# One block around an attention and feed-forward kernel, ordered with the tool's other timing model

## The chip, the cores and the metric

The kernel runs on one core of one Trainium2 chip. The metric is the time of one execution on the device, in microseconds, as the median of several executions.

## The reference

Block-causal attention for 8 batches with 8 heads, 576 positions and 64 columns per head, and behind it a feed-forward layer over all 8 x 576 = 4608 tokens, with 512 columns in and out and 2048 between. Scores are masked in blocks of 64: a position sees its own block and those before it. The weights of the feed-forward arrive as 64-bit floats.

```python
scores = scale * np.matmul(q, k.transpose(0, 1, 3, 2))
scores = np.where(block_i >= block_j, scores, -1000000000.0)
scores = scores - np.max(scores, axis=-1, keepdims=True)
attn = np.exp(scores)
attn = attn / (np.sum(attn, axis=-1, keepdims=True) + 1e-09)
x = np.matmul(attn, v)        # then heads side by side: (4608, 512)
h = x @ w_in
g = np.where(h >= 1, h, np.where(h <= -1, 0.0, (h + 1) ** 2 / 4.0))
out = g @ w_out
```

## The kernel before, in words

Three pieces of work are written as Python generators, and a loop at the end of the function interleaves them.

Attention goes by pairs of heads: 8 batches x 4 pairs = 32 pairs, eight steps each (`attention_steps`). A pair's q and k are loaded in natural layout (`load`, L276 to L300), split into a high and a low part on DVE and POOL (`split_q` L310 and L311, `split_k` L320 and L321, `split_v` L335 and L336), and turned by PE transposes (`turned`, matmul L346; ACT copies the result out at L351, and a DMA at L357 copies one half to other partitions; the last block has L365, L370 and L371). `scores` multiplies (L391 and L394), takes the row maximum on DVE (L414), the exponential with its sum on ACT (L418), and scales on DVE (L400, L401, L424); `scores_last` does the same for the last block (L438 to L450). From the second batch on, the scaled scores `pr` are copied by a DMA into a tile of the type that PE transposes faster (`as_float32r`, L239 for the second batch and L246 behind it). `turn` and `turn_last` transpose them (L461, or L463 in the first batch) and copy them out on ACT and DVE (L454, L456). `weighted` multiplies with v (L500), and the result becomes `xh` and `xl`, the high and low parts of the feed-forward's input (L522, L523, L535, L536, L565, L566). The first two batches use simpler forms of some of these steps.

The feed-forward goes by 9 chunks of 512 tokens, and in each by 16 blocks of 128 of the 2048 columns. `ffn_in` runs twelve matmuls into one PSUM bank (L646), then the activation over ACT, DVE, DVE, ACT and POOL (L655, L656, L659, L660, L661), and loads the block's second weights (L663). `ffn_out` runs eight and four matmuls into four banks (L670, L675); behind the last block of a chunk the banks are copied out (L683, L685) and stored (L687). A chunk can begin only when the attention of its tokens' batch is done, for all four pairs.

The weights are prepared in 64 pieces of 128x256 (`convert`): a load (L160), two steps on ACT (L165, L166), three on DVE (L167, L170, L173), an addition on POOL (L179), a copy on ACT (L181), a subtraction on POOL (L183), and for the second weights a store to DRAM (L209). The pieces are used from the first chunk on.

The order. The loop at the end draws one attention step, then some weight pieces, and from step 36 on one step of the feed-forward (`ffn_in` or `ffn_out` in turn). So from then on a batch of attention stands beside a chunk of the feed-forward: chunk 0 beside batch 1, up to chunk 6 beside batch 7; chunks 7 and 8 come alone. This written order isn't yet that of the chip. The ordering tool runs the traced program in a simulated time of its own: on each engine, and on the queue of SP, which issues all DMAs, it takes the instruction written earliest among those that are ready by its timing model. What comes out is one fixed list for each engine, which the engine then works off in order, waiting at each instruction for the semaphores that the tool has put there. How good the lists are depends on how near the tool's timing model is to the chip. Buffers are few in places: one bank for `ph`, four for `po`, three for the other PSUM tiles (and `po` banks too, in the first 36 steps), two buffers each for `t`, `gh`, `gl` and `wo`.

Of the kernel before, what the change touches and what calls it, by code (L numbers as in the profile page):

```python
# [23 lines left out]
def block_attn_then_ffn(  # L24
# [59 lines left out]


    ident_f = ffn.tile([P, 512], F32, tag="t", name="ident_f")[:, :P]
    make_identity(nc, ident_f)
    ident_r = const.tile([P, P], F32R, tag="ident", name="ident_r")
    nc.vector.tensor_copy(ident_r, ident_f)
    ident = ident_r.bitcast(F32)  # L90

    xh = const.tile([P, NCC, RING], F32R, tag="xh", name="xh")
    xl = const.tile([P, NCC, RING], F32R, tag="xl", name="xl")
    wih = const.tile([P, NCC, DF], F32R, tag="wih", name="wih")
    wil = const.tile([P, NCC, DF], F32R, tag="wil", name="wil")
    wo_split = dram.tile([NFC, P, 2, DM], F32, tag="wo_split", name="wo_split")
# [3 lines left out]
    qa = const.tile([P, 2, QW], F32R, tag="qa", name="qa")  # L100
    qb = const.tile([P, 2, QW], F32R, tag="qb", name="qb")
    ka = const.tile([P, 2, S], F32R, tag="ka", name="ka")
    kb = const.tile([P, 2, S], F32R, tag="kb", name="kb")

    def last_blocks(t_):

        view = t_[:, :, SM : SM + BLK]
        if t_.shape[2] == S:
            return view
        part, (_, two), cols = view.ap  # L110
        return bass.AP(tensor=view.tensor, offset=view.offset, ap=[part, [QW + BLK, two], cols])


    mrow = att1.tile([NTL, 2, S], F32R, tag="pb0", name="mrow")


    pcs = [const.tile([P, 2, BLK], F32R, tag=f"pcs{i}", name=f"pcs{i}") for i in range(2)]
    vsr = [const.tile([P, NTL + 1, 2, D], F32R, tag=f"vsr{j}", name=f"vsr{j}") for j in range(2)]

    mtmp = ffn.tile([P, 512], F32, tag="t", name="mtmp")  # L120
    msel = ffn.tile([P, 512], F32, tag="t", name="msel")
    nc.vector.memset(mtmp, 0.0)
    nc.vector.memset(msel[:NTL], 0.0)
    nc.gpsimd.affine_select(
        out=msel[:NTL, : NTL * BLK].rearrange("p (t c) -> p t c", c=BLK),
        in_=msel[:NTL, : NTL * BLK].rearrange("p (t c) -> p t c", c=BLK),
        compare_op=ALU.not_equal, fill=1.0, base=0,
        pattern=[[-1, NTL], [0, BLK]], channel_multiplier=1,
    )
    sel = msel[:NTL, : NTL * BLK].rearrange("p (t c) -> p t c", c=BLK)  # L130
    for side in range(2):
        nc.vector.tensor_copy(mrow[:, side, :512], mtmp[:NTL, :512])
        nc.vector.tensor_copy(mrow[:, side, 512:S], mtmp[:NTL, : S - 512])
    rows = mrow[:, :, :SM].rearrange("p s (t c) -> p s t c", c=P)
    nc.vector.tensor_copy(rows[:, 0, :, :BLK], sel)
    nc.vector.tensor_scalar_mul(rows[:, 1, :, BLK:], sel, MASKED)
    for t_ in (qa, qb):
        nc.vector.tensor_copy(
            t_[:, :, SM:], mtmp[:, : 2 * (QW - SM)].rearrange("p (h c) -> p h c", h=2)
        )  # L140
    for t_ in pcs:
        nc.vector.tensor_copy(t_[BLK:], mtmp[BLK:, : 2 * BLK].rearrange("p (h c) -> p h c", h=2))
    for t_ in vsr:
        nc.vector.tensor_copy(
            t_[BLK:, NTL, :, :], mtmp[BLK:, : 2 * D].rearrange("p (h c) -> p h c", h=2)
        )
    for j in range(2):
        nc.sync.dma_start(qa[D:KA, j, :S].bitcast(F32), mrow[:, 0, :].bitcast(F32))
        nc.sync.dma_start(ka[D:KA, j, :].bitcast(F32), mrow[:, 1, :].bitcast(F32))


    def convert(n, source, hi, lo, done):

        if n < BORROW and n % 2:
            bits = ffn.tile([P, CW, 2], I32, tag="t", name="bits")
            work = ffn.tile([P, 2, CW], F32, tag="gl", name="work")
        else:
            bits = conv.tile([P, CW, 2], I32, tag="bits", name="bits")
            work = conv2.tile([P, 2, CW], F32, tag="work", name="work")
        nc.sync.dma_start(bits, source.bitcast(I32).rearrange("p (n t) -> p n t", t=2))  # L160
        top, mag = work[:, 0, :], work[:, 1, :].bitcast(U32)
        low = bits[:, :, 0]


        nc.scalar.mul(top, bits[:, :, 1].bitcast(F32), 2.0**-112)  # L165
        nc.scalar.mul(low, low.bitcast(U32), 2.0**-29)  # L166
        nc.vector.tensor_scalar(  # L167
            out=top, in0=top, scalar1=F32_TOP, scalar2=-F32_TOP, op0=ALU.min, op1=ALU.max
        )
        nc.vector.tensor_scalar(  # L170
            out=mag, in0=top.bitcast(U32), scalar1=3, scalar2=None, op0=ALU.logical_shift_left
        )
        nc.vector.scalar_tensor_tensor(  # L173
            out=mag, in0=top.bitcast(U32), scalar=0x80000000, in1=mag,
            op0=ALU.bitwise_and, op1=ALU.bitwise_or,
        )
        yield
        w32 = mag.bitcast(I32)
        nc.gpsimd.tensor_tensor(out=w32, in0=w32, in1=low, op=ALU.add)  # L179
        w32 = w32.bitcast(F32)  # L180
        nc.scalar.copy(hi(), w32)  # L181
        yield
        nc.gpsimd.tensor_tensor(out=lo(), in0=w32, in1=hi().bitcast(F32), op=ALU.subtract)  # L183
        if done:
            done()

    def weight_pieces():

        for f0 in range(0, DF, CW):
            fs = slice(f0, f0 + CW)  # L190
            for cc in range(NCC):
                yield (
                    w_in[cc * P : (cc + 1) * P, fs],
                    lambda cc=cc, fs=fs: wih[:, cc, fs], lambda cc=cc, fs=fs: wil[:, cc, fs], None,
                )
            for fc in range(f0 // P, (f0 + CW) // P):
                ws = {}

                def part(w, d0, ws=ws):
                    if not ws:  # L200
                        ws[0] = ffn.tile([P, 2, DM], F32R, tag="wo", name="ws")
                    return ws[0][:, w, d0 : d0 + CW]

                for d0 in range(0, DM, CW):
                    yield (
                        w_out[fc * P : (fc + 1) * P, d0 : d0 + CW],
                        lambda p_=part, d0=d0: p_(0, d0), lambda p_=part, d0=d0: p_(1, d0),
                        None if d0 + CW < DM else
                        lambda fc=fc, ws=ws: nc.sync.dma_start(wo_split[fc], ws[0].bitcast(F32)),  # L209
                    )  # L210

    def prepare_weights():

        live = []
        for n, piece in enumerate(weight_pieces()):
            live = [c for c in live + [convert(n, *piece)] if next(c, True) is None]
            yield
        for _ in range(LAG):
            live = [c for c in live if next(c, True) is None]
            yield  # L220
# [3 lines left out]
    spare = {"n": 0, "of": []}  # L224

    def as_float32r(src, plain):

        if plain:
            if not spare["of"]:
                spare["of"] = [t_[:, :NTL, :, :].rearrange("p t h d -> p (t h d)") for t_ in vsr]  # L230
                spare["of"].append(att1.tile([P, S], F32R, tag="x32", name="prs")[:, :TCH])
                spare["end"] = att1.tile([P, G0 + P], F32R, tag="pa11", name="pre")[:, :BLK]
            moved = [spare["of"][spare["n"] % 3]]
            spare["n"] += 1
            if src.shape[1] > TCH:
                moved.append(spare["end"])
            for i, dst in enumerate(moved):
                n = min(TCH, src.shape[1] - i * TCH)
                nc.sync.dma_start(dst[:, :n].bitcast(F32), src[:, i * TCH : i * TCH + n])  # L239
            return moved  # L240
        moved = []
        for c0 in range(0, src.shape[1], TCH):
            n = min(TCH, src.shape[1] - c0)
            pool, tag = ((conv, "bits"), (conv2, "work"))[c0 > 0]
            dst = pool.tile([P, TCH], F32R, tag=tag, name="prr")
            nc.sync.dma_start(dst[:, :n].bitcast(F32), src[:, c0 : c0 + n])  # L246
            moved.append(dst)
        return moved


    class Pair:


        GROUPS = (((0, 0), (1, P)), ((2, 0),), ((3, 0),))

        def __init__(self, b, hp):
            self.b, self.hp = b, hp

            self.plain = b < PLAIN
            self.first = b == 0 and hp == 0  # L260

# [467 lines left out]
    for _ in ffn_steps:  # L729
        pass  # L730
# [30 lines left out]
```

## Time and profile before

| | us |
|---|---|
| median of 3 runs | 1271.27 (1271.11 to 1272.6) |
| the profiled execution | 1272.09 |
| its span, first to last instruction | 1270.3 |
| PE busy in the span | 1210.7 (95%) |
| DVE busy | 856.4 (67%) |
| ACT busy | 701.3 (55%) |
| POOL busy | 456.3 (36%) |

The engines are PE (matmuls; PEld are its weight loads), DVE, ACT, POOL, and SP, whose queue issues the DMAs. A row of the timeline has the start, the duration, the engine, the line, the operation, the tile written and those read, the shape, and in square brackets how long the engine stood idle before it and which instruction released it. A row of the waits has the engine and line that waited, for whom, the total in us, how often, and the longest. The granted clock is that of PE as a share of full speed. The mean over the span is 0.985.

### The profile page before, as it was taken

To read this page: it belongs to the slowest core of one execution; us is meant where nothing else is said; L and a number is where in the kernel's file an instruction comes from. 1 tells how busy PE (TensorE), PEld (TensorE's weight loads), DVE (VectorE), ACT (ScalarE), POOL (GpSimd) and SP (SyncE) were. 2 spreads that over 40 slices of the span, in tenths; PEclk is the share of its full clock that TensorE was granted. 3 is DMA by queue.
4 is the path that set the end of the run, shared out by engine and by line. 5 is a ranking of instruction groups with operands and counts; after the bars stand their busy time and mean duration, and the time that the engine had idled before them with its cause. 6 is when DMAs were issued, how large, how long until landed. Compare 5 with 4: busy or idle time off the path is not lost.

```text
span 1270.3 us, 20591 instructions
## 1 busy us (share of the span) xinstructions
PE 1210.7 (95%) x6496; PEld 1018.4 (80%) x6496; DVE 856.4 (67%) x2164; ACT 701.3 (55%) x1827; POOL 456.3 (36%) x454
## 2 busy tenths in 40 slices
PE   5879887899999999999999999999999999999998
PEld 4667666688888888888888888888888888888886
DVE  8998877857776777777777777777777676222222
ACT  5877656546565655566556656555565564222222
POOL 3555655523332333333333333333333332222222
PEclk9888989899999999999999999999999999999999
DMA  5656666655444545564455545454445443322432
GB/s 157 182 165 213 196 228 210 212 184 173 148 152 147 191 144 161 158 193 149 148 162 168 178 141 161 153 181 143 152 154 184 151 132 117 127 92 97 133 100 100
DMA packets 146093, 201.30 MB, mean 158 GB/s; under 512 B 63152, under 2 KB 93872, under 8 KB 145984
## 3 DMA queue, kind: packets, MB, share of 16 engines
q1 hardware_dynamic: 145984, 199.98, 50.4%
q8 instruction: 52, 0.85, 0.3%
q14 instruction: 57, 0.47, 0.1%
HBM read 120.59 MB, written 17.83 MB: 109 GB/s over the span
## 4 chain that ended last, share of the span: by engine, by line
PE 68%; DVE 8%; ACT 4%; issue 3%; DMA 3%; POOL 2%; SPq 0%; ACTq 0%; POOLq 0%; DVEq 0%
PE ph L646 26%; PE po L670 16%; PE po L675 8%; PE ps_av L500 7%; PE ps_t L461 3%; PE ps_s L394 3%; PE ps_s L391 3%; ACT pr L418 2%; PE ps_qk L346 2%; DMA prr<-pr 2%; DVE t L656 2%; DVE nm L414 1%; DVE t L659 1%; DVE pr L424 1%; POOL work L179 1%
## 5 line engine op out<-in xcount | busy, mean ns | idle before, releaser
L661 POOL TENSOR_TENSOR gl<-t,gh 128x512 fp32r<-128x512 f32 x144 | 186.9, 1298 | 604.7 <-ACT gh L660 301.8
L670 PE MATMUL po<-wo,gh 128*128 128x512 f32 x1152 | 296.9, 399 | 0.1
L656 DVE SCALAR_TENSOR_TENSOR t<-t 128x512 f32<-128x512 f32 x144 | 112.9, 784 | 200.2 <-ACT t L655 198.5
L646 PE MATMUL ph<-xh,wih 128*128 128x512 f32 x576 | 237.6, 413 | 2.7 <-DVE t L659 1.8
L670 PEld LDWEIGHTS po<-wo,gh 128*128 128x128 f32 x1152 | 207.7, 188 | 39.3 <-ACT gh L660 0.6
L646 PE MATMUL ph<-xl,wih 128*128 128x512 f32 x576 | 227.4, 395 | 0.9 <-DVE xl L536 0.9
L646 PE MATMUL ph<-xh,wil 128*128 128x512 f32 x576 | 227.4, 395 | 0.0
L655 ACT ACTIVATE t<-ph 128x512 f32<-128x512 f32 x144 | 86.1, 598 | 184.7 <-PE ph L646 184.7
L418 ACT ACTIVATE pr<-ps_s,nm 128x128 f32<-128x128 f32 (+3 forms) x256 | 134.4, 529 | 50.6 <-DVE nm L414 50.3
L414 DVE TENSOR_REDUCE nm<-ps_s 128x1 f32<-128x128 f32 (+3 forms) x256 | 123.6, 485 | 48.7 <-PE ps_s L394 47.4
L675 PE MATMUL po<-wo,gl 128*128 128x512 f32 x576 | 155.3, 391 | 0.0
L660 ACT CAST gh<-t 128x512 fp32r<-128x512 f32 x144 | 89.6, 622 | 102.1 <-DVE t L659 101.7
L391 PE MATMUL ps_s<-ka,qa 68*128 68x288 f32 (+4 forms) x384 | 122.5, 334 | 9.1 <-ACT kb L351 4.2
L646 PEld LDWEIGHTS ph<-xh,wil 128*128 128x128 f32 x576 | 109.1, 189 | 24.1
L675 PEld LDWEIGHTS po<-wo,gl 128*128 128x128 f32 x576 | 108.1, 188 | 23.3
L646 PEld LDWEIGHTS ph<-xh,wih 128*128 128x128 f32 x576 | 109.1, 189 | 21.7 <-DVE t L659 2.4
L646 PEld LDWEIGHTS ph<-xl,wih 128*128 128x128 f32 x576 | 109.6, 190 | 20.2 <-DVE xl L536 1.5
L394 PE MATMUL ps_s<-kb,qb 128*128 128x288 f32 (+4 forms) x384 | 121.4, 323 | 0.0
L454 ACT CAST pb<-ps_t 128x512 fp32r<-128x512 f32 (+1 forms) x120 | 65.5, 546 | 85.6 <-PE ps_t L461 83.8
L424 DVE TENSOR_SCALAR pr<-pr,sm 128x128 f32<-128x128 f32 (+3 forms) x256 | 104.8, 430 | 4.0
L336 POOL TENSOR_TENSOR vsr<-vn,vsr 64x64 fp32r<-64x64 f32 (+1 forms) x96 | 72.8, 768 | 88.6 <-ACT vsr L335 88.6
L456 DVE TENSOR_TENSOR pb<-ps_t,pb 128x512 fp32r<-128x512 f32 (+1 forms) x120 | 75.6, 630 | 40.4 <-ACT pb L454 39.9
(101 smaller groups left out, 1961.4 us busy)
## 6 DMA issues: line engine op xcount, KB each, us to landing
wo<-wo_split SPq DMA_DIRECT2D x144, 512.0 KB, 3.4
prr<-pr SPq DMA_DIRECT2D x96, 192.0 KB, 2.7
prr<-pr SPq DMA_DIRECT2D x72, 256.0 KB, 2.6
out_dram<-ob SPq DMA_DIRECT2D x36, 256.0 KB, 3.9
qn<-in_q_dram SPq DMA_DIRECT2D x32, 256.0 KB, 2.9
kn<-in_k_dram SPq DMA_DIRECT2D x32, 256.0 KB, 2.9
bits<-in_moe_w_in_dram SPq DMA_DIRECT2D x32, 256.0 KB, 3.6
bits<-in_moe_w_out_dram SPq DMA_DIRECT2D x32, 256.0 KB, 3.2
```

The costliest lines, as they stand in the source:

```text
L391: nc.tensor.matmul(ps, qa[:KA, j, c0 : c0 + P], ka[:KA, j, k0 : k0 + n], start=first, stop=False)
L394: nc.tensor.matmul(ps, qb[:, j, c0 : c0 + P], kb[:, j, k0 : k0 + n], start=False, stop=last)
L414: nc.vector.tensor_reduce(out=nm[:, i : i + 1], in_=ps[:, cs], axis=AX.X, op=ALU.max, negate=True)
L418: nc.scalar.activation(pr[:, cs], ps[:, cs], AF.Exp, bias=nm[:, i : i + 1], scale=1.0, accum_out=sm[:, i : i + 1],)
L424: nc.vector.tensor_scalar_mul(pr[:, cs], pr[:, cs], sm[:, i : i + 1])
L500: nc.tensor.matmul(ps[:, lo_col:], vt, x, start=first and i == 0 and m == 0, stop=last and i == len(parts) - 1 and m == len(mov) - 1,)
L646: nc.tensor.matmul(ph, w[:, cc, fs], x[:, cc, xs], start=(cc == 0 and i == 0), stop=(cc == NCC - 1 and i == 2),)
L656: nc.vector.scalar_tensor_tensor(out=t_, in0=t_, scalar=1.0, in1=t_, op0=ALU.min, op1=ALU.mult)
L660: nc.scalar.copy(gh, t_)
L661: nc.gpsimd.tensor_tensor(out=gl, in0=t_, in1=gh.bitcast(F32), op=ALU.subtract)
L670: nc.tensor.matmul(po[tt], gh[:, ts_], wo[:, w, :], start=(fc == 0 and w == 0), stop=False)
L675: nc.tensor.matmul(po[tt], gl[:, ts_], wo[:, 0, :], start=False, stop=fc == NFC - 1)
```

## The change

The whole body of the function, from the first tile to the last step of the feed-forward, is put into one block, and the block is given the flag that makes the tool order it with its other timing model, which describes the machine in more detail. The tile pools stay outside. No instruction, shape, buffer or loop is changed; the rest of the diff is indentation, and each line behind the new one has a number higher by one.

```diff
-
-    ident_f = ffn.tile([P, 512], F32, tag="t", name="ident_f")[:, :P]
-    make_identity(nc, ident_f)
+    with tc.block(schedule_with_timeline_sim=True):
+
+        ident_f = ffn.tile([P, 512], F32, tag="t", name="ident_f")[:, :P]
+        make_identity(nc, ident_f)
...
-    for _ in ffn_steps:
-        pass
+        for _ in ffn_steps:
+            pass
```

More of the change, by code (lines that the diff above doesn't have):

```diff
@@ L95, in block_attn_then_ffn @@
[L95 to L111, printed above, removed]
@@ L141, in block_attn_then_ffn @@
[L141 to L185, printed above, removed]
@@ L212, in prepare_weights @@
[L212 to L248, printed above, removed]
@@ L496, in weighted @@
-        def weighted(self, ps, j, parts, first=True, last=True):
-            for i, (kt, lo_col, mov) in enumerate(parts):
-                vt = self.vs[j][: (BLK if self.plain and kt == NTL else P), kt, :, :]
-                for m, x in enumerate(mov):
-                    nc.tensor.matmul(
-                        ps[:, lo_col:], vt, x,
-                        start=first and i == 0 and m == 0,
-                        stop=last and i == len(parts) - 1 and m == len(mov) - 1,
-                    )
@@ L666, in ffn_out @@
-    def ffn_out(po, c, fc, gh, gl, wo):
-        for tt in range(NTT):
-            ts_ = slice(tt * P, (tt + 1) * P)
-            for w in range(2):
-                nc.tensor.matmul(
-                    po[tt], gh[:, ts_], wo[:, w, :], start=(fc == 0 and w == 0), stop=False
-                )
-        for tt in range(NTT):
-            ts_ = slice(tt * P, (tt + 1) * P)
-            nc.tensor.matmul(po[tt], gl[:, ts_], wo[:, 0, :], start=False, stop=fc == NFC - 1)
-        if fc < NFC - 1:
-            return
-        for tt in range(NTT):
-            ob = conv.tile([P, DM], F32, tag="bits", name="ob") if tt % 2 else conv2.tile(
-                [P, DM], F32, tag="work", name="ob"
-            )
-            if tt % 2:
-                nc.scalar.copy(ob, po[tt])
-            else:
-                nc.vector.tensor_copy(ob, po[tt])
-            r0 = c * TCH + tt * P
-            nc.sync.dma_start(out[r0 : r0 + P, :], ob)
@@ new lines, in ffn_in @@
+        def ffn_in(c, fc):
+            at = (c * TCH) % RING
+            ph = ps_h.tile([P, 512], F32, tag="ph", name="ph")
+            fs = slice(fc * P, (fc + 1) * P)
+            xs = slice(at, at + TCH)
+            for cc in range(NCC):
+                for i, (w, x) in enumerate(((wih, xh), (wih, xl), (wil, xh))):
+                    nc.tensor.matmul(
+                        ph, w[:, cc, fs], x[:, cc, xs],
+                        start=(cc == 0 and i == 0), stop=(cc == NCC - 1 and i == 2),
+                    )
+            t_ = ffn.tile([P, TCH], F32, tag="t", name="t")
+            gh = ffn.tile([P, TCH], F32R, tag="gh", name="gh")
+            gl = ffn.tile([P, TCH], F32R, tag="gl", name="gl")
+            nc.scalar.activation(t_, ph, AF.Relu, bias=0.5, scale=0.5)
+            nc.vector.scalar_tensor_tensor(
+                out=t_, in0=t_, scalar=1.0, in1=t_, op0=ALU.min, op1=ALU.mult
+            )
+            nc.vector.tensor_tensor(out=t_, in0=ph, in1=t_, op=ALU.max)
+            nc.scalar.copy(gh, t_)
+            nc.gpsimd.tensor_tensor(out=gl, in0=t_, in1=gh.bitcast(F32), op=ALU.subtract)
+            wo = ffn.tile([P, 2, DM], F32R, tag="wo", name="wo")
+            nc.sync.dma_start(wo.bitcast(F32), wo_split[fc])
+            return gh, gl, wo
@@ new lines, in ffn_out @@
+        def ffn_out(po, c, fc, gh, gl, wo):
+            for tt in range(NTT):
+                ts_ = slice(tt * P, (tt + 1) * P)
+                for w in range(2):
+                    nc.tensor.matmul(
+                        po[tt], gh[:, ts_], wo[:, w, :], start=(fc == 0 and w == 0), stop=False
+                    )
+            for tt in range(NTT):
+                ts_ = slice(tt * P, (tt + 1) * P)
+                nc.tensor.matmul(po[tt], gl[:, ts_], wo[:, 0, :], start=False, stop=fc == NFC - 1)
+            if fc < NFC - 1:
+                return
+            for tt in range(NTT):
+                ob = conv.tile([P, DM], F32, tag="bits", name="ob") if tt % 2 else conv2.tile(
+                    [P, DM], F32, tag="work", name="ob"
+                )
+                if tt % 2:
+                    nc.scalar.copy(ob, po[tt])
+                else:
+                    nc.vector.tensor_copy(ob, po[tt])
+                r0 = c * TCH + tt * P
+                nc.sync.dma_start(out[r0 : r0 + P, :], ob)
@@ new lines, in feed_forward @@
+        def feed_forward():
+            prev = None
+            for c in range(NCH):
+                for fc in range(NFC):
+                    cur = (c, fc, *ffn_in(c, fc))
+                    yield
+                    if prev is not None:
+                        if prev[1] == 0:
+                            po = [ps_o.tile([P, DM], F32, tag="po", name="po") for _ in range(NTT)]
+                        ffn_out(po, *prev)
+                        yield
+                    prev = cur
+            ffn_out(po, *prev)
+            yield
```

923 lines of the change are left out of this document (489 added, 434 removed).

## The prediction

> **What bounds the kernel now.** I read the totals first, then the busy time of the engines stretch by stretch, with the borders set where the work changes: start, first batch of attention, first chunk of the feed-forward with the weights still being prepared, six batches side by side with six chunks, and two chunks alone. The columns are: stretch in us, its length, busy us of PE, PEld, DVE, ACT, POOL with counts, granted clock, DMA share, GB/s.
>
> ```profile
> span 1270.3 us, 20591 instructions
> ```
> ```profile
> 0.00:13.00 13.00, 2.81 (x20) 2.62 (x20) 8.48 (x27) 4.02 (x9) 1.73 (x9) 1.00 0.52 131
> 13.00:100.00 87.00, 71.05 (x365) 57.68 (x365) 80.20 (x247) 68.92 (x212) 47.46 (x58) 0.88 0.60 178
> 100.00:275.00 175.00, 154.26 (x756) 121.23 (x756) 135.65 (x342) 108.83 (x309) 95.03 (x112) 0.95 0.67 212
> 275.00:1085.00 810.00, 802.35 (x4572) 688.70 (x4571) 582.64 (x1478) 476.44 (x1229) 269.32 (x242) 1.00 0.50 157
> 1085.00:1270.00 185.00, 180.19 (x791) 148.19 (x789) 49.40 (x72) 43.05 (x72) 42.76 (x34) 1.00 0.33 108
> ```
>
> From 275 us on, PE is the bound: it stands idle for 810.00 - 802.35 = 7.65 us of 810, and in the last stretch only at the very end. An order can win nothing there except these 7.65 us. The time that an order could still win lies before 275 us. In 13 to 100 PE is idle for 15.95 us, but DVE is busy for 80.20 of 87, so this stretch can shrink by 6.8 us at most. In 100 to 275 PE is idle for 20.74 us and no other engine is full (DVE 135.65 of 175).
>
> To that comes a clock below 1 in the same two stretches. Six shorter stretches hold nearly all of it:
>
> ```profile
> 45.50:57.00 11.50, 7.72 (x43) 6.92 (x43) 10.17 (x31) 8.37 (x26) 7.28 (x9) 0.70 0.50 144
> 68.00:79.00 11.00, 8.57 (x48) 7.46 (x49) 10.14 (x31) 8.56 (x28) 5.97 (x9) 0.69 0.56 170
> 91.00:103.00 12.00, 10.53 (x54) 8.94 (x53) 10.03 (x33) 9.19 (x29) 7.06 (x9) 0.72 0.61 185
> 111.00:117.00 6.00, 4.25 (x14) 3.29 (x14) 5.82 (x19) 3.85 (x13) 2.75 (x3) 0.72 0.69 222
> 157.00:165.00 8.00, 6.67 (x29) 4.91 (x28) 6.53 (x18) 5.74 (x18) 5.06 (x7) 0.79 0.70 223
> 218.00:228.00 10.00, 6.02 (x21) 4.56 (x20) 7.34 (x21) 6.11 (x19) 4.78 (x6) 0.71 0.77 246
> ```
>
> My estimate of what the slow clock costs is busy PE time by the missing share: 2.3 + 2.7 + 2.9 = 7.9 us before 100, and 1.2 + 1.4 + 1.7 = 4.3 us after. So the stretch from 100 to 275 holds 20.74 + 4.3 = 25.0 us of idle and slowed PE.
>
> **What the present order looks like.** In the steady stretch the matmuls run in the order in which the code is written. One piece of a pair, in order of time:
>
> ```profile
> 804.26 0.51 PE L346 MATMUL ps_qk<-ident_r,qs 128*128 128x128 f32 x4
> 804.60 0.46 PE L646 MATMUL ph<-xh,wih 128*128 128x512 f32 x1
> ...
> 807.21 0.39 PE L646 MATMUL ph<-xh,wil 128*128 128x512 f32 x1
> 807.44 0.22 PE L391 MATMUL ps_s<-ka,qa 68*128 68x128 f32 x1
> ...
> 808.21 0.50 PE L461 MATMUL ps_t<-ident_r,prr 128*128 128x128 f32 x4
> 808.54 2.08 PE L670 MATMUL po<-wo,gh 128*128 128x512 f32 x8
> 810.46 1.08 PE L675 MATMUL po<-wo,gl 128*128 128x512 f32 x4
> 811.37 0.35 PE L391 MATMUL ps_s<-ka,qa 68*128 68x384 f32 x1
> ```
>
> This is one attention step, `ffn_in`, the next attention step, `ffn_out`, and the next, as the loop at the end of the kernel writes them. I matched the k-th matmul of each kind with the k-th of that kind as written, over the whole trace: from 275 to 1085, 236 of 4570 stand at another place (one group of four transposes per pair, moved behind a few `ffn_in` matmuls); after 1085 none of 789; but 282 of 363 from 13 to 100, and 237 of 754 from 100 to 275. The tool leaves the written order only where, in its own clock, PE would otherwise have nothing to do. So a second timing model changes the order where PE is not full, mostly before 275 us, and has little to change behind it.
>
> **The change, part by part.** No instruction's shape, tile, buffer or DMA is added or removed. Moved is, on every engine and on SP's queue, which ready instruction goes first, and the whole program stands in a block that is entered once.
>
> First, the stalls made by the order. An engine takes its queue in order, so a wrong guess of the tool costs time when an instruction that isn't ready stands ahead of one that is. The clearest one:
>
> ```profile
> 217.13 0.39 PE L646 MATMUL ph<-xh,wil 128*128 128x512 f32 x1
> ...
> 217.82 0.46 PE L346 MATMUL ps_qk<-ident_r,ks 128*128 128x128 f32 x4
> ...
> 221.08 0.40 ACT L181 CAST ws<-work 128x256 fp32r<-128x256 f32 x1 [1.99 <-POOL work L179]
> 221.39 0.59 ACT L655 ACTIVATE t<-ph 128x512 f32<-128x512 f32 x1
> ...
> 221.88 0.58 ACT L351 CAST kb<-ps_qk 128x512 fp32r<-128x512 f32 x1
> ...
> 222.51 0.69 PE L391 MATMUL ps_s<-ka,qa 68*128 68x384 f32 x1 [3.89 <-ACT kb L351]
> ```
>
> The matmuls that L655 and L351 read ended at 217.5 and 218.3, yet both run after 221: ahead of them on ACT stands L181, a copy of the weight preparation, which waits 1.99 us for POOL. PE stands still for 3.89 us and then runs at a clock of 0.71 (1.7 us by the row above), 5.6 us together. This wait is no single case:
>
> ```profile
> ACT wih L181 <- POOL work L179: 18.5, 17, 3.2
> ACT ws L181 <- POOL work L179: 12.6, 14, 2.0
> ```
>
> ACT stands 31.1 us in this one wait, 31 times. In most of them nothing that PE needs is queued behind. A model that times the chain DVE, POOL, ACT better would put L655 and L351 first at 218 us. What is late next is DVE, which is busy for 7.34 us of the ten from 218 to 228: if all its work has to stay there, the gain ends at 2.7 us; if some moves into the rest of the stretch, it reaches 5.6. I take the middle, 4.1 us.
>
> The second large stall is on DVE:
>
> ```profile
> 47.06 1.04 DVE L167 TENSOR_SCALAR work<-work 128x256 f32<-128x256 f32 x1
> ...
> 48.09 0.74 DVE L167 TENSOR_SCALAR work<-work 128x256 f32<-128x256 f32 x1
> 48.75 0.51 DVE L450 TENSOR_SCALAR pr<-pr,sm 128x576 f32<-128x576 f32 x1
> ```
> ```profile
> 49.41 1.30 PE L463 MATMUL ps_t<-ident_r,pr 128*128 128x128 f32 x5 [3.78 <-DVE sm L400]
> ```
>
> Two steps of the weight preparation, 1.04 + 0.74 = 1.78 us, stand ahead of the scaling L450 that PE waits 3.78 us for. Put behind it, they would shorten the stall by 1.78 us; but DVE is busy for 10.17 of the 11.5 us from 45.5 to 57, so I take 11.50 - 10.17 = 1.3 us.
>
> The other idle times of PE before 275 us are many and small; a new order takes some away and makes others, and I put them at nothing, with all the rest (6.8 + 25.0 us, and 7.65 behind) as the bound of a gain: 39.5 us. Their loss is priced as a rival.
>
> The clock: a rule of the Trainium skill bears on what a short stall costs. The trace shows a slow stretch behind a short gap:
>
> ```profile
> 68.70 1.09 PE L463 MATMUL ps_t<-ident_r,pr 128*128 128x128 f32 x4 [1.63 <-ACT pr L444]
> ```
>
> The gap is 1.63 us and the clock of 68 to 79 is 0.69. The Trainium skill, "TensorE: Matmul & The Clock Gate", section "Part 1: The HAM clock gate (the "warmup" mystery)", has PE fall to half its clock after an idle window of about 3.4 us. Taken as the length of a gap, only the stalls of 3.78 and 3.89 us would be followed by a slow clock, and the 12.2 us of slowed PE time would be 2.3 + 1.7 = 4.0; the trace does not agree, so I keep 12.2.
>
> Second, the block. The trace of before shows no entry of a block. Each engine goes there once and comes out once. The nearest row is that of fetched instructions:
>
> ```profile
> q8 instruction: 52, 0.85, 0.3%
> ```
>
> 0.3% of 16 engines' span over 52 packets is 0.003 x 1270.3 x 16 / 52 = 1.2 us for one. An entry that finds its instructions at hand costs nothing; one that has to fetch them, at the start and again at the end, costs 2.4 us. A gain is excluded, since nothing is left out for it. I take one fetch, 1.2 us, as the engines enter together and at the end wait for the last output anyway. The Trainium skill, "Runtime: NRT & Kernel Launch", section "Instruction fetch mechanics", speaks for the upper end: a taken branch to a page that isn't loaded stalls until it is fetched. By that the term would be 2.4 us and the forecast 1.2 us later.
>
> Sum: -4.1 - 1.3 + 1.2 = -4.2 us. The profiled execution took 1272.1 us, 1.8 more than its span, and stands 0.8 above the median of the runs, 1271.3. So the span would be 1266.1, that execution 1267.9, and a median run 1267.1, 0.33% less. A measurement here tells 0.2%, 2.5 us, from no change.
>
> **The rivals.** *Nothing that can be measured.* For it: 810 + 185 of the 1270 us run PE full in the order as written, and greedy filling only moves idle time about; before 275 us gains and losses may cancel. Against it: the two stalls above are large and made by the order alone. Also, if the block were ordered as before, only the entry would be left. Time: 1271.3 to 1272.5, say 1272.
>
> *Slower in the steady stretch.* The new model may take the way of the scaled scores through DMA (L246) as quicker than it is, and put the transposes that read them (L461) ahead of the feed-forward group that now covers the way.
>
> ```profile
> 802.11 0.47 SPq L246 DMA_DIRECT2D prr<-pr  x1
> ```
> ```profile
> prr<-pr SPq DMA_DIRECT2D x96, 192.0 KB, 2.7
> ```
> ```profile
> PE ps_t L461 <- DMA prr<-pr: 3.2, 5, 1.6
> ```
>
> This copy is issued at 802.11, lands about 2.7 us later, at 804.8, and is read at 808.21: 3.4 us to spare, a little more than the twelve matmuls from 804.60 to 807.44 take (2.8 us). If the transposes are drawn ahead by more than that, PE waits; such a wait is now 3.2 / 5 = 0.64 us on average and comes five times. Once in each of the 24 pairs of this stretch it makes 24 x 0.64 = 15.4 us, with the entry 1287.9. For it: what costs a little here counts 24 times. Against it: PE is full there, and with a full PE the tool keeps the written order.
>
> *Slower before 275 us.* The new model may guess the weight chain worse, and put L181 in front of something PE needs at more places than at 218 us. Two more such stalls make 2 x 5.6 us, with the entry 1283.7. For it: L181 waits 31 times already, and only few of these stop PE. It decides from the second new stall on; one is paid by the gain.
>
> **How the numbers follow.** The forecast, a gain from the two stalls or others of their size, has 0.42: it needs a model that is better where the present one is wrong, which the two stalls allow and don't prove. No measurable change has 0.25, since most of the time is bound by a full PE. Slower in the steady stretch has 0.18, slower before 275 us 0.15, together 0.33. The range goes down to half of the bound of 39.5 us, 1271.3 - 19.8 = 1251.5, and up to the steady rival, 1288. The forecast case alone ranges from 1251.5 to 1268.7.
>
> **What would show it right or wrong.** Right: the gap of about 3.9 us before a PE L391 and that of 3.8 us before L463 are gone or under 2 us, the wait of L181 for L179 is well under 31 us, PE's clock from 13 to 275 is above the present 0.88 and 0.95, and the time is won before 275 us while the six batches behind take as long as before. The first matmul would start 1.2 us later than now, for the entry. Wrong: a steady stretch whose PE idle time grows from 7.65 to over 15 us, waits of L461 for the copied scores at many pairs, or first stretches in which the idle time only changes its place.

## The result, and the profile after

The changed kernel takes 1447.2 us (median, 1441.69 to 1447.61) against 1271.93 us (1271.11 to 1273.57) for the kernel before on the same chip: a ratio of 1.1372, 95% interval 1.1353 to 1.1391. The forecast was 1267.1 us with a range up to 1288. The profiled execution took 1446.92 us.

The totals and the two rows by slices of the page after:

```profile
span 1444.7 us, 20660 instructions
...
PE 1313.1 (91%) x6496; PEld 1088.3 (75%) x6496; DVE 876.0 (61%) x2164; ACT 700.4 (48%) x1827; POOL 445.1 (31%) x454
...
PE   5788988999987999799998999789987999799998
...
PEclk8789999999986999679985999699976999599999
```

The span grew by 174.4 us: PE is busy for 102.4 us more (1313.1 - 1210.7) with the same matmuls, and idle for 72.0 us more. PE's clock dips at regular distances (6, 6, 5, 6, 6, 5), once per batch, 4 to 5 slices of 36 us apart. The same stages as in the prediction, the third and fourth border moved to where the work changes now:

```profile
13.00:100.00 87.00, 61.24 (x274) 49.57 (x275) 79.83 (x225) 65.68 (x198) 53.49 (x67) 0.73 0.65 203
100.00:275.00 175.00, 155.43 (x783) 124.70 (x782) 131.21 (x331) 103.50 (x290) 85.98 (x101) 0.96 0.61 188
275.00:1260.00 985.00, 914.19 (x4659) 765.16 (x4658) 608.76 (x1514) 485.31 (x1261) 261.68 (x246) 0.88 0.43 134
1260.00:1444.00 184.00, 176.73 (x759) 144.46 (x758) 46.78 (x68) 41.08 (x68) 42.08 (x33) 0.97 0.30 98
```

The six batches with a chunk beside them took 810 us with 7.65 idle at full clock; they now take 985 with 70.8 idle (985.00 - 914.19) at 0.88. The two lone chunks take what they took. Cut finer, the long stage alternates between full and bare stretches:

```profile
350.00:400.00 50.00, 50.00 (x269) 42.44 (x268) 30.70 (x73) 24.43 (x64) 15.35 (x14) 1.00 0.44 138
400.00:450.00 50.00, 41.14 (x214) 33.98 (x213) 31.65 (x85) 26.18 (x73) 10.76 (x12) 0.81 0.38 114
...
750.00:800.00 50.00, 41.58 (x176) 34.11 (x176) 32.72 (x93) 26.73 (x72) 10.22 (x11) 0.58 0.41 122
800.00:850.00 50.00, 50.00 (x269) 42.48 (x269) 32.49 (x71) 24.60 (x62) 15.16 (x15) 1.00 0.46 144
```

What PE does in a full stretch (first rows) and in a bare one (last rows, from the batch before), from the timeline:

```profile
565.23 0.52 PE L462 MATMUL ps_t<-ident_r,prr 128*128 128x128 f32 x5
565.59 0.45 PE L671 MATMUL po<-wo,gh 128*128 128x512 f32 x1
565.88 1.08 PE L676 MATMUL po<-wo,gl 128*128 128x512 f32 x4
566.80 0.39 PE L647 MATMUL ph<-xh,wih 128*128 128x512 f32 x1
...
569.54 1.99 PE L671 MATMUL po<-wo,gh 128*128 128x512 f32 x8
571.37 0.46 PE L347 MATMUL ps_qk<-ident_r,ks 128*128 128x128 f32 x4
571.67 0.47 PE L392 MATMUL ps_s<-ka,qa 68*128 68x512 f32 x1
```
```profile
432.49 0.51 PE L347 MATMUL ps_qk<-ident_r,qs 128*128 128x128 f32 x4 [1.04 <-DVE pb L457]
...
435.37 0.82 PE L462 MATMUL ps_t<-ident_r,prr 128*128 128x128 f32 x5 [1.81 <-DVE sm L402]
435.99 0.69 PE L347 MATMUL ps_qk<-ident_r,ks 128*128 128x128 f32 x4
437.40 0.79 PE L392 MATMUL ps_s<-ka,qa 68*128 68x512 f32 x1 [0.72 <-ACT kb L352]
```

In the full stretch the end of one `ffn_out`, a whole `ffn_in` (the first of its twelve matmuls is shown) and the eight of another `ffn_out` stand between the transposes of one attention step (L462) and the multiplication of the next (L392), where the program writes a single feed-forward step. So the feed-forward runs ahead. Counted as in the prediction, 3847 of 3851 matmuls from 275 to 1085 us stand at another place than written (before 236 of 4570); the lead grows from 0 to 12 or 13 of a chunk's 32 steps. Then the chunk is used up, and the next one needs the x of the batch that isn't done. The last twelve or so attention steps run with nothing beside them, and PE waits for DVE and ACT at every step.

The length of a batch is read from the last matmul of L500 (after: L501) of each batch, with the batches counted from 1 to 8. Those of batches 2 and 7, before and after:

```profile
273.49 0.43 PE L500 MATMUL ps_av<-pc,vs 64*128 64x64 f32 x2
...
947.75 0.33 PE L500 MATMUL ps_av<-pcs,vsr 128*128 128x64 f32 x2
```
```profile
294.16 0.43 PE L501 MATMUL ps_av<-pc,vs 64*128 64x64 f32 x2
...
1101.96 0.52 PE L501 MATMUL ps_av<-pcs,vsr 128*128 128x64 f32 x2
```

Five batches take (948.1 - 273.9) / 5 = 134.8 us before and (1102.5 - 294.6) / 5 = 161.6 after: 26.7 each, 134 us together. Another 21 us are lost by the end of batch 2 (294.6 against 273.9; 16 of them by the end of batch 1, 122.7 against 106.3), and 21 in the last batch (155 against 134). With the tail, which is 1.3 us shorter, that is the whole.

### The profile page after: what moved, and what is told of

It reads as the page before. It is cut to its first block, busy times and chain, and to the rows that moved or that the text cites. A ratio compares the mean times of both kernels' runs of the same rounds, so it can differ in the third digit from the quotient of the medians.

```text
span 1444.7 us, 20660 instructions
## 1 busy us (share of the span) xinstructions
PE 1313.1 (91%) x6496; PEld 1088.3 (75%) x6496; DVE 876.0 (61%) x2164; ACT 700.4 (48%) x1827; POOL 445.1 (31%) x454
## 4 chain that ended last, share of the span: by engine, by line
PE 72%; DVE 7%; DMA 5%; ACT 4%; issue 2%; SPq 1%; POOL 1%; ACTq 0%; DVEq 0%; POOLq 0%
PE ph L647 27%; PE po L671 18%; PE po L676 9%; PE ps_av L501 7%; PE ps_s L392 4%; PE ps_s L395 3%; PE ps_t L462 3%; PE ps_qk L347 2%; DMA prr<-pr 2%; DMA bits<-in_moe_w_out_dram 1%; DVE nm L415 1%; DMA wo<-wo_split 1%; ACT pr L419 1%; DVE pb L457 1%; DVE x L524 1%
## 5 line engine op out<-in xcount | busy, mean ns | idle before, releaser
L671 PE MATMUL po<-wo,gh 128*128 128x512 f32 x1152 | 314.6, 400 | 5.2 <-DMA wo<-wo_split 4.4
L657 DVE SCALAR_TENSOR_TENSOR t<-t 128x512 f32<-128x512 f32 x144 | 102.9, 714 | 241.3 <-ACT t L656 241.3
L647 PE MATMUL ph<-xl,wih 128*128 128x512 f32 x576 | 235.3, 409 | 0.9 <-POOL xl L567 0.9
L392 PE MATMUL ps_s<-ka,qa 68*128 68x288 f32 (+4 forms) x384 | 150.4, 402 | 17.8 <-ACT pr L419 4.9
L676 PE MATMUL po<-wo,gl 128*128 128x512 f32 x576 | 166.4, 398 | 0.0
L395 PE MATMUL ps_s<-kb,qb 128*128 128x288 f32 (+4 forms) x384 | 136.4, 360 | 0.0
L425 DVE TENSOR_SCALAR pr<-pr,sm 128x128 f32<-128x128 f32 (+3 forms) x256 | 119.2, 489 | 4.3
L337 POOL TENSOR_TENSOR vsr<-vn,vsr 64x64 fp32r<-64x64 f32 (+1 forms) x96 | 59.4, 627 | 198.1 <-ACT vsr L336 183.1
L392 PEld LDWEIGHTS ps_s<-ka,qa 68*128 68x128 f32 x384 | 86.3, 225 | 32.6 <-ACT pr L419 8.1
L462 PEld LDWEIGHTS ps_t<-ident_r,prr 128*128 128x128 f32 x600 | 74.0, 153 | 41.8 <-issue 11.7
```

The costliest lines, as they stand in the source:

```text
L392: nc.tensor.matmul(ps, qa[:KA, j, c0 : c0 + P], ka[:KA, j, k0 : k0 + n], start=first, stop=False)
L395: nc.tensor.matmul(ps, qb[:, j, c0 : c0 + P], kb[:, j, k0 : k0 + n], start=False, stop=last)
L425: nc.vector.tensor_scalar_mul(pr[:, cs], pr[:, cs], sm[:, i : i + 1])
L462: nc.tensor.transpose(out.bitcast(F32R), src, ident_r)
L647: nc.tensor.matmul(ph, w[:, cc, fs], x[:, cc, xs], start=(cc == 0 and i == 0), stop=(cc == NCC - 1 and i == 2),)
L657: nc.vector.scalar_tensor_tensor(out=t_, in0=t_, scalar=1.0, in1=t_, op0=ALU.min, op1=ALU.mult)
```

## The experiments

"Batch" is the mean length of batches 3 to 7, read as above.

| kernel | us | ratio to before, 95% interval | batch, us |
|---|---|---|---|
| before | 1271.9 | | 134.8 |
| changed | 1447.2 | 1.137 (1.135 to 1.139) | 161.6 |
| block, old model | 1270.9 | 1.000 (0.999 to 1.001) | |
| feed-forward held, new / old model | 1355.0 / 1288.4 | 1.066 (1.063 to 1.068) / 1.015 (1.013 to 1.017) | 147.3 / 136.9 |
| every eighth step held, new | 1395.6 | 1.099 (1.098 to 1.101) | 153.5 |
| lead by hand, old | 1374.6 | 1.081 (1.078 to 1.083) | 153.2 |
| new model up to step 36 | 1293.2 | 1.017 (1.015 to 1.019) | 134.7 |
| PE as written, new / old | 1364.1 / 1333.5 | 1.072 (1.070 to 1.075) / 1.050 (1.047 to 1.052) | 147.7 / 142.8 |
| PE in the old order, new / old | 1341.5 / 1273.4 | 1.054 (1.051 to 1.057) / 1.002 (1.001 to 1.004) | 143.8 / 134.3 |
| the same, late weights, new / old | 1298.0 / 1287.4 | 1.023 (1.020 to 1.027) / 1.015 (1.012 to 1.019) | 136.6 / 136.5 |
| no copy of the scores, new / old | 1414.3 / 1279.3 | 1.112 (1.109 to 1.115) / 1.007 (1.005 to 1.008) | 157.6 / 136.1 |

`keep_in_program_order` holds an instruction behind all that is written ahead of it on its engine.

**The block alone.**

```diff
-    with tc.block(schedule_with_timeline_sim=True):
+    with tc.block():
```

> The whole program in a block, ordered with the old model. Lead theory (the new model lets the feed-forward run ahead of the attention on PE, its chunk is used up early, and the end of each batch of attention runs with nothing beside it): the block is not the cause, 1272 to 1275 us. Block theory (the block itself costs the time, by its entry and its fetched instructions): about 1447 us.

1270.92 us: the block costs nothing that can be measured, so all is the model's.

**The feed-forward held back, under both models.**

```diff
-                    nc.tensor.matmul(
+                    mm = nc.tensor.matmul(
                         ph, w[:, cc, fs], x[:, cc, xs],
...
+                    if cc == 0 and i == 0:
+                        tc.keep_in_program_order(mm)
```

(and the same at the first matmul of `ffn_out`)

> The changed kernel, but the first matmul of each ffn_in and ffn_out may not pass PE work that is written ahead of it; all else, on every engine, is still ordered by the new model. Lead theory: no chunk is used up early, the batches with a chunk beside them go back from about 160 to about 135 us each, and only the loss of the first batch (about 17 us) is left: 1280 to 1300 us. Rival (the new order of ACT, DVE, POOL and SP slows the attention, and PE's order only shows it): still over 1400 us.

> Control: the kernel before, old model, with the same hold on the first matmul of each ffn_in and ffn_out. Lead theory: the feed-forward never led there, so the hold changes little: batches of 134 to 138 us, 1270 to 1300 us. Rival (the hold itself costs, and made the 13 us a batch that were left with it under the new model): batches of about 147 us, about 1350 us.

1354.97 us lies between the two. The lead in PE's order is gone (at most 2 steps) and the bare stretches with it, which wins 14 us a batch; but 147.3 us is still 10 above the same hold under the old model, 136.9 (1288.37 us, as expected). So the lead is not all.

**The lead by itself, in two doses.**

```diff
+                    if fc % 8 == 0 and cc == 0 and i == 0:
+                        tc.keep_in_program_order(mm)
```
```diff
-            next(ffn_steps, None)
+            n = (i - START) % (2 * NFC)
+            ahead = i >= START + 2 * NFC
+            upto = lambda m: max(m, min(2 * NFC - 2, m * 8 // 5))
+            todo = upto(n + 1) - upto(n) if ahead else 1
+            for _ in range(todo):
+                next(ffn_steps, None)
```

(The first, under the new model, holds blocks 0 and 8 of each chunk, at `ffn_in` and in the same way at `ffn_out`; the second, under the old model, writes the feed-forward ahead.)

> The changed kernel with only every eighth feed-forward step held back, so that the lead can grow to 4 steps, twice a batch, instead of 12 once (and 2 with each step held back). Lead theory: the loss grows with the steps that are left bare, so this lies between 1355 and 1447 us: 1380 to 1420 us. Rival (only a long bare stretch costs, a short one is covered by what the attention has ready): 1350 to 1370 us.

> The kernel before with its old model, but the feed-forward is written ahead: from the second chunk on 8 feed-forward steps are issued with each 5 attention steps until 30 of the 32 are out, so the lead grows to 10 steps, and the last ten or so attention steps of a batch stand alone, in six batches. Lead theory: this alone makes most of the loss, 6 x 15 to 25 us, so 1360 to 1420 us. Rival (the other engines' new order is what costs; on PE the same work is only moved): 1272 to 1290 us.

Both came as the lead theory has it, 1395.62 and 1374.56 us. In the first the lead reaches about 5 steps, twice a batch, where 4 were expected. Written by hand into the old model's kernel, a lead of 10 steps costs 18 us a batch and makes the same picture stretch by stretch:

```profile
475.00:525.00 50.00, 50.00 (x271) 42.49 (x270) 32.03 (x74) 23.96 (x59) 14.23 (x13) 1.00 0.47 147
525.00:575.00 50.00, 44.31 (x251) 37.21 (x250) 31.20 (x87) 27.57 (x74) 11.82 (x12) 0.92 0.44 138
575.00:625.00 50.00, 46.85 (x231) 39.44 (x231) 34.00 (x85) 27.51 (x72) 14.06 (x14) 0.81 0.41 128
```

**The new model for the first stage alone.** The block ends ahead of step 36; the loop goes on outside it.

> The new model for everything up to attention step 36 (first batch, before the feed-forward begins), the old one for all behind. Lead theory: the steady batches take 134.5 us as before, and what is left is the first batch's loss of 17 us with perhaps a few us for the border: 1280 to 1300 us. Rival (a disturbed start is handed on from batch to batch): batches of about 160 us, about 1440 us.

1293.22 us, batches of 134.7: a bad start costs its own 22 us (1293.22 - 1270.8) and isn't handed on.

**PE as written.** Every PE instruction is wrapped in `keep_in_program_order`; then all but the transposes of L347; then, instead, the first matmuls of the feed-forward and all of ACT and DVE.

> The changed kernel with every PE instruction kept in the order in which it is written; ACT, DVE, POOL and SP are ordered by the new model. With only the feed-forward held back a batch took 147 us, 13 more than before, and this run asks where these 13 come from. PE theory (PE's order inside the attention and inside the feed-forward groups): batches of 134 to 136 us, total 1272 plus the first batch's loss, 1275 to 1300 us. Rival (the new order of ACT, DVE, POOL and SP delays what PE waits for): batches still 145 us or more, 1340 to 1370 us.

> Control: the kernel before, old model, every PE instruction in written order. From 275 us on it is in written order nearly everywhere already, so the batches should take 134.5 us as before; in the first batch PE may no longer step over what isn't ready, which costs 0 to 40 us: 1272 to 1312 us. If written order on PE itself were worth something in the steady stretch, batches would be under 134 us.

> The changed kernel with every PE instruction in written order except the transposes of q and k (L347), which the new model may place. With PE wholly in written order a batch took 143 us under the old model and 147 us under the new one, and PE waited at these transposes for L419 (the exponential that frees their PSUM bank). Theory (of these, 8 to 9 us a batch are the place of these transposes, which the old model moves behind a few feed-forward matmuls): batches of about 139 us, the other engines' order costing the remaining 4, total 1310 to 1335 us. Rival (the new model doesn't move them, or not to where it helps): batches still 145 us or more, 1350 to 1370 us.

> The changed kernel with the first matmul of each ffn_in and ffn_out held back as before and ACT and DVE wholly in written order; PE inside the attention, POOL and SP are left to the new model. PE theory: batches still about 147 us, 1335 to 1370 us. Rival (ACT and DVE): batches of about 135 us, 1272 to 1300 us.

With the feed-forward held, a batch under the new model was still 13 us longer than before (147.3 against 134.8). With all of PE as written it takes 147.7 us (1364.12 us), so the new order of the other engines has a part in the 13 us. But against the expectation it takes 142.8 under the old model too (1333.48 us): 8 us more than with the old model's own order, which in the steady stretch differs from the written one in four transposes per pair. PE's wait there from 275 to 1085 us, with PE as written under the old model:

```profile
PE ps_qk L346 <- ACT pr L418: 34.1, 22, 1.9
```

Leaving L347 free under the new model gave nothing (1367.42 us, batches of 150.3; the theory failed): it does not move them, and from 300 to 1050 us PE works in the written order throughout. And ACT and DVE in written order are worse than in any model's (1583.52 us, batches of 170.5), so that run can't tell which of their steps the new model misplaces.

**PE in the old order, under both models.** The four transposes are written where the old model puts them, and all of PE is held.

```diff
-                nxt.turned(False, 0)
+                late.append(nxt)
             yield
+            flush()
             cur.scores(1, 2)
...
+                if cc == 2 and i == 0:
+                    flush()
```

(`flush` calls `turned(False, 0)`; the last two lines stand in `ffn_in` behind its matmul)

> The changed kernel with every PE instruction in written order, and the four transposes of the next pair's k written where the old model puts them, behind the seventh matmul of the next ffn_in. ACT, DVE, POOL and SP are ordered by the new model. If the 13 us a batch are PE's order inside the attention: batches of 134 to 137 us, 1285 to 1305 us with the loss of the first batches. If they are partly the other engines' order (4 us, as the two runs with PE in written order differ): 138 to 141 us, 1310 to 1335 us. If they are all the other engines': 145 us or more, over 1350 us.

> Control under the old model, the same fixed PE order. Theory (the place of these four transposes is the 9 us a batch that PE's written order cost under the old model): batches of 134 to 136 us, 1280 to 1300 us. Rival (the 9 us came from other places): batches still about 143 us, about 1333 us.

Under the old model the place of four transposes is the whole 8 us: 134.3 us a batch, 1273.44 us. With PE's order the same in both, the new order of the other engines and of SP's queue costs 9.4 us a batch (143.8, 1341.53 us), between the two cases of the expectation, about 4 and 13. PE's waits from 300 to 1050 us in the two kernels, new model first:

```profile
PE ps_t L462 <- DMA prr<-pr: 25.2, 16, 3.0
PE ps_t L462 <- DVE t L666: 11.2, 7, 1.8
```
```profile
PE ps_t L461 <- DMA prr<-pr: 1.7, 3, 0.9
PE ps_t L461 <- DVE t L665: 1.0, 1, 1.0
```

The wait falls once in nearly every pair on the same group of four transposes, 1.1 to 3.0 us. The waits put down to L666 belong to it as well: in all 20 waits of over 1 us the transposes start 0.14 us after the copy has landed. One of them, and SP's queue ahead of it, new model first, then the queue under the old one:

```profile
817.92 0.50 PE L462 MATMUL ps_t<-ident_r,prr 128*128 128x128 f32 x4 [1.74 <-DMA prr<-pr]
```
```profile
812.15 1.57 SPq L673 DMA_DIRECT2D wo<-wo_split  x1
813.82 0.50 SPq L247 DMA_DIRECT2D prr<-pr  x1
```
```profile
825.19 0.54 SPq L246 DMA_DIRECT2D prr<-pr  x1
825.83 0.54 SPq L672 DMA_DIRECT2D wo<-wo_split  x1
```

The load of the output weights, 512 KB, stands ahead of the copy of the scores under the new model and behind it under the old one. In each of the 20 waits the copy that is waited for was issued right behind such a load, and it landed 3.9 to 5.9 us after its issue began. Over all copies of the scores (L247, under the old model L246) the shortest, median and longest are, new model first:

```profile
DMA to landing us min/median/max: 2.0/2.3/5.9
```
```profile
DMA to landing us min/median/max: 1.9/2.7/4.0
```

**That load issued one attention step later, under both models.**

```diff
-        nc.sync.dma_start(wo.bitcast(F32), wo_split[fc])
+        wait_wo.append((wo, fc))
...
+            tc.keep_in_program_order(nc.sync.dma_start(wo.bitcast(F32), wo_split[fc]))
```

> The new model with PE's order fixed to the old one, and the load of the output weights for each feed-forward step issued one attention step later, so that on SP's queue it stands behind the copy of the scores. Theory (the load ahead of the copy is what costs 9 us a batch): the wait of L462 for the copy goes from once a pair to a few, batches of 134 to 137 us, 1285 to 1305 us with the loss of the first batches. Rival (the order on ACT and DVE): batches of 141 us and more, over 1325 us.

> Control under the old model, PE's order the same, the load as late. There the copy stands ahead of the load already. Theory: nothing changes, batches of 134 to 135 us, 1270 to 1280 us. Rival (the later load comes too late for its matmuls): PE waits for wo, over 1285 us.

The difference between the models is gone from the batches: 136.6 us under the new one (1297.97 us), 136.5 under the old (1287.42 us; here the control's rival held). The totals still differ by 10.6 us, and that is there by the end of batch 2 (289.8 against 279.3 us). Behind 300 us this kernel has the same order on PE, DVE, ACT and POOL as the one under the new model without the late load, and that order still differs from the old model's on DVE (640 of 1535 instructions) and ACT (471 of 1290). On SP's queue, besides the load, the copy has changed places with one load of k in 20 pairs. So the rival, the order on ACT and DVE, is excluded, and SP's queue is what cost the 9.4 us. Both pay 2 us for the load itself, which now comes late. The wait for the copy is no longer among PE's waits of the new model's kernel from 275 to 1085 us (L687 are matmuls of `ffn_out`):

```profile
PE po L687 <- DMA wo<-wo_split: 14.5, 22, 1.5
```

**The copy left out.**

```diff
-    HOP = 1
+    HOP = 8
```

> The changed kernel without the scores' way through DMA: they are transposed as plain float32, which takes PE longer. Theory (the new model takes that way as longer than the old one does, finds the attention late and fills in with the feed-forward): without it no lead, and the time is within 3% of the same kernel under the old model. Rival (the lead has another cause): a lead of 10 to 14 steps as in the changed kernel, and 8 to 16% more than under the old model.

> Control: the kernel before without the scores' way through DMA, old model. Both theories: no lead, PE full in the steady batches; 24 pairs with longer transposes, estimated from 1.30 us for five plain ones against 0.53 us for five copied ones as 25 x 0.15 us a pair, so 1272 + 24 x 3.9 = 1365 us.

The lead is there without the copy too, and the loss to the control is 21.5 us a batch instead of 26.7. So the copy is not why the feed-forward gets ahead; in the changed kernel what hangs on it is worth about 5 us of the 27. The control missed its estimate by far: 1279 us instead of 1365. The 1.30 us had come from a stretch with a slow clock; at full clock five plain transposes take 0.71 us:

```profile
700.32 0.71 PE L463 MATMUL ps_t<-ident_r,pr 128*128 128x128 f32 x5
```

**The first batch.** The conversion of the weights is held back with the feed-forward, under the new model; and, with the new model only up to step 36, the conversion alone.

```diff
+            tc.keep_in_program_order(st)
```

(behind each of the conversion's steps on ACT, DVE and POOL)

> The feed-forward held back, and the conversion of the weights too: its steps on ACT, DVE and POOL may not pass work written ahead of them. In the first batch of the changed kernel 23 pieces of weights are begun on DVE by 75 us, where before it was 18. Theory (the new model lets whatever isn't urgent run ahead, the weights in the first batch like the feed-forward later): the first batch ends near 120 us again instead of 136, and the total is 12 to 20 us under the 1355 with the feed-forward alone held back. Rival (the first batch is slow because of the order inside the attention): total within 5 us of 1355.

> The new model up to attention step 36 and the old one behind, with the conversion of the weights held back to written order. With the conversion held back under the new model the first batch ended at 99.7 us and the second at 261.3, against 106.3 and 273.9 before. Theory (in the first batch the conversion takes DVE, ACT and POOL away from the attention, and an order that lets it wait wins that): 1258 to 1270 us, faster than before. Rival (the conversion is due before the second batch's feed-forward anyway, and the time is given back there): 1270 to 1290 us.

The first batch ends at 99.7 us instead of 125.8 with the feed-forward alone held: the weights running ahead are its loss. (By the reading of batches used here it ended at 106.3 us in the kernel before, so the 120 and 136 us of the expectation are not on this scale.) But the totals are 1364.23 and 1298.78 us, no better than without (1354.97 and 1293.22). The held weights seem to come due in the next batches: batch 3 took 183 us in the first kernel (149 with the feed-forward alone held), batch 2 took 203 in the second (178 without the hold). The first theory was right that the batch gets shorter and wrong on the total. Of the second the rival's mechanism fits, but the time lies over its range, which ended at 1290 us. No run here beat the kernel before.

## Why the prediction was wrong

*The step that failed:* "So a second timing model changes the order where PE is not full, mostly before 275 us, and has little to change behind it." PE's 7.65 us of idle time in 810 were read as the bound of what an order can do there. They bound a gain; they say nothing of a loss. PE was full because of its order: taking the written one, nearly the same, costs 8 us a batch, and a lead 18.

*How the tool reorders.* From one trace it was concluded that the written order is left only where PE would have nothing to do. That may well hold of the new model too, in its own clock. But the prediction took PE full on the chip as PE full in that clock. It has no row for what the second model thinks, and the small share of displaced matmuls came from the first.

*The stalls before 275 us, -4.1 and -1.3.* The first part came true: ACT's wait in L182 for POOL fell from 31.1 us to 12.7, and the longest wait before L392 (L391 before) from 3.89 to 2.45.

```profile
ACT wih L182 <- POOL work L180: 7.2, 8, 1.7
ACT ws L182 <- POOL work L180: 5.5, 7, 1.5
```

The gain did not follow. New stalls took their place; two of the longest, from PE's timeline of the changed kernel:

```profile
28.72 1.30 PE L464 MATMUL ps_t<-ident_r,pr 128*128 128x128 f32 x5 [5.30 <-DVE pr L451]
...
39.33 1.09 PE L464 MATMUL ps_t<-ident_r,pr 128*128 128x128 f32 x4 [3.05 <-DVE pr L425]
```

From 13 to 100 us PE idles for 25.8 us (87.00 - 61.24) instead of 15.95, and its clock is 0.73 instead of 0.88; from 100 to 275 little changed. In the first batch DVE begins 23 pieces of weights by 75 us, before 18.

*The block, +1.2.* The block alone stands at a ratio of 0.9998 (0.9985 to 1.0012), that is -1.9 to +1.5 us: 1.2 us isn't excluded, but nothing speaks for it. The 2.4 us that the prediction put beside the rule of the Trainium skill ("Runtime: NRT & Kernel Launch", "Instruction fetch mechanics") lie outside. Nor does the first matmul start 1.2 us later, as the prediction's sign has it: 7.10 us into the span with the block alone, 7.58 before.

*The rivals.* "Slower in the steady stretch" had the place and the sign, not the mechanism or the size: 15.4 us, by transposes drawn ahead on PE. In the changed kernel PE waits for the copies for 13.8 us in all. "Slower before 275 us" happened as well, 21 us, by the conversion ahead of the attention as a rule, not by two more stalls.

*What is shown and what stays open.* Shown: the lead alone makes 18 us a batch in the old kernel, and holding it back wins 14 in the new one; with PE's order equal, the place of one load on SP's queue makes the 9.4 us that were left between the two models. Not shown: how the 26.7 of the changed kernel divide, since its PE order is another and what is left with the hold (with the hold, under the new model, from 275 to 1170 us: three short waits a pair, 46.6 us in all, the rows below) stands at other places; and which price in the new model makes the attention seem late.

```profile
PE ps_av L501 <- DVE pb L457: 17.3, 23, 0.8
PE ps_qk L347 <- ACT pr L419: 16.3, 23, 1.5
PE po L673 <- ACT gh L663: 13.0, 23, 0.6
```

## What to carry to other kernels

A full engine bounds what a new order can win, not what it can lose: ask which independent work is finite and what covers the rest once it is used up. Filler that may run ahead (here the feed-forward) has to be tied to the work that it covers, and a bulk load has to be kept behind the small transfer that somebody waits for. Neither is free: under the old model, whose order was good already, holding the feed-forward made 1288.4 us of 1271.9 and the late load 1287.4 us of 1273.4, and holding the weights back won nothing in total. Before a whole program is handed to another ordering, compare the two orders: how far the filler leads is seen there without any time.

## What the runs showed of the hardware

The clock falls without a long gap. From 750 to 800 us of the changed kernel it is 0.58, and the longest idle time of PE in that stretch is this one:

```profile
764.30 0.83 PE L462 MATMUL ps_t<-ident_r,prr 128*128 128x128 f32 x5 [2.87 <-DMA prr<-pr]
```

An estimate from the stage: 914.19 us busy with 0.12 of the clock missing are 110 us, about the 102.4 that PE's busy time grew. So the larger part of the loss is work at a slow clock, and not the waits themselves. That short waits bring the slow clock on is inferred: in the rows of 50 us above, of the changed kernel and of the lead by hand, PE is busy for all 50.00 us where the clock is 1.00, and for 41.14 to 46.85 us where it is 0.58 to 0.92; no run here changes the one without the other. The Trainium skill, "TensorE: Matmul & The Clock Gate", section "A second HAM failure mode: psum-queue depth-cycling", tells of a kernel whose clock swings because PE idles briefly between groups of matmuls; the trace agrees as far as that goes.

The way of the scores through DMA, made for the sake of quicker transposes, is worth little: without it the kernel before takes 1.0067 of its time (1.005 to 1.0084).

A copy issued right behind a 512 KB load on the same queue lands late: 3.9 to 5.9 us after its issue in the 20 waits above, where the median over all such copies of that kernel is 2.3 us.
